# A recurrent attention loop with streamed weights: new fixed order, V and O in parts, mask on TensorE, half of the KT and QT copies on ScalarE

## The chip, the cores and the metric

The kernel runs on one core of one Trainium2 chip. The time is the device time of a whole execution in microseconds (us). All runs told here are fast; each is compared by its ratio to runs of the kernel before of the same rounds on the same chip. The profile is one execution taken by the hardware profiler.

In this kernel TensorE does the matmuls and transposes and writes them to PSUM; VectorE (DVE in the profile), ScalarE (ACT) and GpSimd (POOL) copy and compute on tiles; SyncE (SP) issues the loads of the weights into SBUF, the on-chip memory. PE in the profile is a matmul, PEld the load of its stationary operand.

## The reference, cut to what matters

Two independent parts are concatenated. Part A (a short convolution and a long one by FFT) is not touched by the change. Part B is recurrent over 64 segments:

```python
for s in range(n_seg):                       # 64 segments of 32 tokens
    h = concat([mem, xs])                    # 8 + 32 = 40 rows, 1024 wide
    q, k, v = h @ Wq, h @ Wk, h @ Wv         # 32 heads of 128
    p = softmax(where(mask, q @ k.T * scale, -1e9))
    o = (p @ v) @ Wo
    mem = o[:, :8]                           # goes into the next segment
    outs.append(o[:, 8:])
```

A segment needs all four weight matrices, 32 MB in bf16, and the next segment needs its result. The mask lets memory rows see everything and is causal otherwise.

## The kernel before

The weights are 64 chunks of 128 x 2048 bf16 (512 KB). 44 stay in SBUF, 20 are streamed again in every segment through a ring of four slots. A slot is loaded again when TensorE is done with it:

```python
NSTREAM = 20        # chunks streamed per segment
RING = 4
...
    def fetch():
        n = len(loaded)
        if n < len(uses):
            t = ring.tile([128, 2048], BF, tag="wring", name="wring")
            nc.sync.dma_start(dst_view(t[:], uses[n]), dram_chunk(uses[n]))
            loaded.append(t)
    ...
    def done(ch):                 # after the matmuls of a chunk
        if ch in streamed:
            loaded[used[0]] = None
            used[0] += 1
            fetch()
```

The heads are done in two halves (g = 0, 1). KT and QT are the transposed keys and queries, S the scores, PT the transposed probabilities, OT the attention output, `acc` and `yacc` the sums of the projections. The order of a segment is fixed by the program text; each engine works its own instructions in that order (the timeline below shows it on VectorE: a copy stands behind a softmax that it does not need, and TensorE waits 1.45 us):

```python
            k0 = evac_qk(proj(0, 0))            # K, half 0: 8 chunks, then a ScalarE copy
            q0 = evac_qk(proj(1, 0))
            KT0 = keys(0)
            transposes(k0, KT0[:, :, :, 0:32])  # TensorE transposes, VectorE copy to SBUF
            k1 = evac_qk(proj(0, 1))
            ...
            transposes(q0, QT0[:])
            q1 = evac_qk(proj(1, 1))
            S0 = scores(0, QT0, KT0)
            PT0 = softmax(S0)                   # VectorE chain with Exp on ScalarE
            KT1 = keys(1)
            transposes(k1, KT1[:, :, :, 0:32])  # its VectorE copy stands behind softmax(S0)
            a_v0 = proj(2, 0)
            ...
            transposes(q1, QT1[:])
            S1 = scores(1, QT1, KT1)
            a_v1 = proj(2, 1)
            ...
            attend(0, PT0, V0, OTp)
            evac_o(0, OTp, OT0)
            ...
            PT1 = softmax(S1)
            ...
            out_proj(0, ...)                    # 8 chunks of Wo, needs OT0 at once
            attend(1, PT1, V1, OTp)
            evac_o(1, OTp, OT1)
            out_proj(1, ...)                    # needs OT1 at once
            Y = ...                             # copy, two transposes, copy into `rec`: the next h
```

There is one PSUM buffer for transposes (`tp`), so the transposes of q1 wait until KT1 was copied out. The softmax works on 4 x 2 blocks of 40 columns: per block of heads one block for the recurrent 32 rows and one, a quarter filled, for the last 8 tokens of a segment:

```python
            def softmax(S):
                nc.vector.scalar_tensor_tensor(out=S4, in0=S4, scalar=scale, in1=mask[...],
                                               op0=ALU.mult, op1=ALU.add)       # mask pass
                nc.vector.tensor_reduce(out=mx[:], in_=S3, op=ALU.max, axis=AX.X)
                nc.vector.tensor_tensor(out=S3, in0=S3, in1=mx[...], op=ALU.subtract)
                nc.scalar.activation(S3, S3, ACT.Exp)
                ... # sum, reciprocal, multiply into P_pad, two 32x32-block transposes into PT
```

## Time and profile before

The median before the change was 2918.79 us (three runs, 2917.12 to 2920.53). The loop over the segments takes 80% of it. The copies of Y on ScalarE mark the segments: the first ends at 603.0 us, the last at 2904.3 us, so a segment takes (2904.3 - 603.0) / 63 = 36.5 us.

| per segment, kernel before | us |
|---|---|
| TensorE busy | 24.6 |
| TensorE idle until a weight load has landed | 6.2 |
| TensorE idle for another engine or its own queue | 5.7 |
| sum | 36.5 |

These are sums over all segments but the first and last five. The waits themselves, in the view of waits for TensorE between 1500 and 2500 us (27.4 segments; the columns are us in total, times, and the longest in us):

```profile
PE acc L616 <- DMA wring<-in_B_Wq_dram: 132.4, 112, 2.8
PE yacc L695 <- ACT OT L683: 43.0, 56, 1.1
PE qk_tp L630 <- DVE KT L631: 36.1, 28, 2.1
PE OTp L673 <- DVE PT L663: 34.4, 21, 2.1
PE acc L616 <- DMA wring<-in_B_Wv_dram: 21.6, 31, 1.6
PE S L637 <- DVE QT L631: 14.5, 28, 0.5
PE y_tp L581 <- ACT Y L741: 12.1, 27, 0.5
PE acc L616 <- DMA wring<-in_B_Wk_dram: 9.3, 11, 1.8
PE acc L616 <- DVE rec L582: 9.2, 27, 0.3
PE yacc L695 <- DMA wring<-in_B_Wo_dram: 6.8, 10, 1.7
```

The rows with `wring` are the weight ring, 170 us in all. OT, KT, PT and QT are dependencies that another order could cover, 128 us or 4.7 us a segment. Y and `rec` are the hand-over to the next segment, which nothing can cover. How the KT wait comes about is seen in the timeline (start, duration, engine; in brackets the idle time before and what ended it):

```profile
1535.92 0.77 DVE L663 STREAM_TRANSPOSE PT<-P_pad 128x256 bf16<-128x256 bf16 x2
1536.62 0.38 DVE L631 COPY KT<-qk_tp 128x512 bf16<-128x512 bf16 x1
1537.06 0.38 PE L630 MATMUL qk_tp<-ident,qk_sb 128*128 128x128 bf16 x4 [1.45 <-DVE KT L631]
```

The copy of KT could have been made long before. It stood behind the end of the softmax (the last transposes into PT are seen) on VectorE, and TensorE waited 1.45 us for the transpose buffer. The same wait one segment earlier took 2.04 us:

```profile
1499.97 0.45 PE L630 MATMUL qk_tp<-ident,qk_sb 128*128 128x128 bf16 x4 [2.04 <-DVE KT L631]
```

The windows view gives, for a stretch, its length, the busy time of PE, PEld, DVE, ACT and POOL, then the granted TensorE clock, the busy share of the DMA engines and the GB/s. First the whole loop, then two single microseconds just after that wait:

```profile
700.00:2500.00 1800.00, 1210.35 (x24686) 639.10 (x24682) 458.14 (x1150) 286.32 (x543) 230.84 (x495) 0.85 0.88 298
...
1501.00:1502.00 1.00, 1.00 (x40) 0.50 (x44) 0.00 (x0) 0.00 (x0) 0.00 (x0) 0.50 1.01 395
1502.00:1503.00 1.00, 1.00 (x16) 0.42 (x12) 0.00 (x0) 0.00 (x0) 0.00 (x0) 0.50 0.41 152
```

While TensorE was held up it freed no slot, so SyncE issued no load of the ring between 1497.8 and 1502.3 us. The loads under way land, and the DMA falls from 395 to 152 GB/s in a microsecond in which TensorE is busy again, here at half clock. Later TensorE catches up and starves. The time from issue to landing of the ring's loads, from the view of the tile `wring` over 1500 to 2500 us:

```profile
DMA to landing us min/median/max: 3.8/5.6/8.2
```

(The trace has the landing of three ring loads in eight.) With 20 loads a segment and 5.6 us each, 20 x 5.6 / 36.5 = 3.1 of the four slots are under way on average.

### The profile page before, as it was taken

To read this page: it belongs to the slowest core of one execution; us is meant where nothing else is said; L and a number is where in the kernel's file an instruction comes from. 1 tells how busy PE (TensorE), PEld (TensorE's weight loads), DVE (VectorE), ACT (ScalarE), POOL (GpSimd) and SP (SyncE) were. 2 spreads that over 40 slices of the span, in tenths; PEclk is the share of its full clock that TensorE was granted. 3 is DMA by queue.
4 is the path that set the end of the run, shared out by engine and by line. 5 is a ranking of instruction groups with operands and counts; after the bars stand their busy time and mean duration, and the time that the engine had idled before them with its cause. 6 is when DMAs were issued, how large, how long until landed. Compare 5 with 4: busy or idle time off the path is not lost. (4 is left out here: it accounts for less than half of the span.)

```text
span 2915.3 us, 75121 instructions
## 1 busy us (share of the span) xinstructions
PE 1911.7 (66%) x33470; PEld 975.6 (33%) x33492; DVE 847.1 (29%) x1940; ACT 577.1 (20%) x1015; POOL 382.4 (13%) x742
## 2 busy tenths in 40 slices
PE   3664698366666666676666666666667666766765
PEld 1221343133333333333333333333333333333333
DVE  6894211022222222222222222222222222222222
ACT  6771111011111111111111111111111111111111
POOL 4141000011111111111111111111111111111111
PEclk9797698688888988888888888888887888788888
DMA  7887655888888888888888889888888888888896
GB/s 244 297 268 277 235 137 164 293 297 293 300 294 302 306 303 295 298 296 299 298 300 288 299 298 315 289 298 297 304 302 301 296 294 292 308 297 292 304 304 227
DMA packets 340398, 830.98 MB, mean 285 GB/s; under 512 B 72076, under 2 KB 84396, under 8 KB 340071
## 3 DMA queue, kind: packets, MB, share of 16 engines
q1 hardware_dynamic: 306520, 767.19, 77.2%
q0 software_dynamic: 23168, 34.77, 3.7%
q10 hardware_dynamic: 10384, 24.20, 2.5%
q8 instruction: 262, 4.29, 0.6%
q14 instruction: 64, 0.52, 0.1%
HBM read 774.52 MB, written 51.38 MB: 283 GB/s over the span
## 5 line engine op out<-in xcount | busy, mean ns | idle before, releaser
L616 PE MATMUL acc<-wring,rec 128*32 128x512 bf16 x3840 | 453.2, 457 | 410.1 <-DMA wring<-in_B_Wq_dram 301.4
L616 PEld LDWEIGHTS <-rec 128*32 128x32 bf16 x12288 | 365.4, 108 | 945.6 <-issue 738.8
L616 PE MATMUL acc<-Wearly,rec 128*32 128x512 bf16 x4608 | 440.8, 465 | 32.8 <-DVE rec L582 21.7
L695 PE MATMUL yacc<-Wlate,OT 128*32 128x256 bf16 x5632 | 307.7, 320 | 97.8 <-ACT OT L683 97.7
L616 PE MATMUL acc<-Wlate,rec 128*32 128x512 bf16 x3840 | 352.7, 438 | 0.0
L624 ACT CAST qk_sb<-acc 128x512 bf16<-128x512 f32 x256 | 149.8, 585 | 1016.9 <-PE acc L616 960.9
L695 PEld LDWEIGHTS <-OT 128*32 128x32 bf16 x8192 | 250.1, 113 | 163.5 <-ACT OT L683 111.4
L631 DVE COPY KT<-qk_tp 128x512 bf16<-128x512 bf16 x128 | 51.8, 404 | 583.5 <-PE qk_tp L630 583.5
L683 ACT CAST OT<-OTp 128x512 bf16<-128x512 f32 x128 | 74.9, 585 | 525.9 <-PE OTp L677 525.9
L630 PE MATMUL qk_tp<-ident,qk_sb 128*128 128x128 bf16 x1024 | 115.7, 244 | 91.1 <-DVE KT L631 91.1
L695 PE MATMUL yacc<-wring,OT 128*32 128x256 bf16 x2560 | 164.8, 325 | 13.6 <-DMA wring<-in_B_Wo_dram 12.4
L684 DVE CAST OTB<-OTp 128x128 bf16<-128x128 f32 x128 | 37.4, 292 | 365.9 <-ACT OT L683 365.9
L574 POOL DMA_DIRECT2D rec<-REC x64 | 37.2, 581 | 810.3 <-PE OTp L677 562.3
L606 POOL COPY KT<-rec 128x128 bf16<-128x128 bf16 x128 | 38.1, 298 | 796.0 <-PE S L641 708.6
L648 DVE SCALAR_TENSOR_TENSOR S<-S,mask 128x320 f32<-128x320 f32 x128 | 63.3, 495 | 239.5 <-PE S L641 239.5
L630 PEld LDWEIGHTS <-qk_sb 128*128 128x128 bf16 x1024 | 71.0, 106 | 183.9 <-issue 175.9
L744 POOL DMA_DIRECT2D out_dram<-Y x64 | 48.2, 752 | 636.3 <-ACT Y L741 588.2
L602 POOL DMA_DIRECT2D VBs<-VBD x256 | 129.2, 511 | 0.3
L631 DVE COPY QT<-qk_tp 128x512 bf16<-128x512 bf16 x128 | 54.3, 424 | 237.6 <-PE qk_tp L630 237.6
L673 PE MATMUL OTp<-PT,V 32*128 32x40 bf16 x2048 | 55.3, 180 | 80.1 <-DVE PT L663 78.7
L663 DVE STREAM_TRANSPOSE PT<-P_pad 128x256 bf16<-128x256 bf16 x256 | 98.7, 424 | 4.4
L695 PE MATMUL ybacc<-Wlate,OTB 128*32 128x256 bf16 x1408 | 92.4, 289 | 5.3 <-ACT V L728 2.7
(258 smaller groups left out, 2090.4 us busy)
## 6 DMA issues: line engine op xcount, KB each, us to landing
wring<-in_B_Wq_dram SPq DMA_DIRECT2D x384, 512.0 KB, 5.4
wring<-in_B_Wv_dram SPq DMA_DIRECT2D x320, 512.0 KB, 5.8
wring<-in_B_Wo_dram SPq DMA_DIRECT2D x320, 512.0 KB, 5.4
wring<-in_B_Wk_dram SPq DMA_DIRECT2D x256, 512.0 KB, 6.1
rec<-REC POOLq DMA_DIRECT2D x64, 192.0 KB, 5.7
SK_61<-s_sb SPq DMA_DIRECT2D x16, 512.0 KB, 4.4
SU_60<-s_sb SPq DMA_DIRECT2D x16, 512.0 KB, 3.7
Kg<-SK_61 ACTq DMA_DIRECT2D x32, 256.0 KB, 4.7
```

The source lines that it names most:

```text
L602: nc.gpsimd.dma_start(VBs[32 * c:32 * c + 8, :], VBD[s, c])
L606: nc.gpsimd.tensor_copy(KT[:, :, :, 32:40], KBs[:, 128 * g:128 * g + 128].rearrange("p (c i t) -> p i c t", c=4, i=4))
L616: nc.tensor.matmul(acc[32 * c:32 * c + 32, :], lhsT=hT[:, kc, :], rhs=w[:, c * 512:(c + 1) * 512], start=(kc == 0), stop=(kc == 7), tile_p ...
L624: nc.scalar.copy(sb[:], acc[:])
L630: nc.tensor.transpose(tp[:, i * 128:(i + 1) * 128], sb[:, i * 128:(i + 1) * 128], ident[:])
L631: nc.vector.tensor_copy(dst, tp[:].rearrange("p (i c r) -> p i c r", i=4, c=4))
L648: nc.vector.scalar_tensor_tensor(out=S4, in0=S4, scalar=scale, in1=mask[:].unsqueeze(1).to_broadcast([128, 4, 2, 40]), op0=ALU.mult, op1=A ...
L663: nc.vector.transpose(out=PT[:, kb].rearrange("p i (a q) -> p (i a) q", a=2), in_=P_pad[:].rearrange("p i a k -> p (i a) k")[:, :, 32 * kb ...
L673: nc.tensor.matmul(OTp[:, c, idx * 40:idx * 40 + 40], lhsT=V[32 * c:32 * c + 32, cv], rhs=PT[32 * c:32 * c + 32, 0, i, 0:40], start=True, ...
L683: nc.scalar.copy(OT[:], v[:, :, :, 0:32])
L695: nc.tensor.matmul(acc[32 * dq:32 * dq + 32, 0:256], lhsT=src[:, c, idx, :], rhs=w[:, hh * 1024 + dq * 256:hh * 1024 + (dq + 1) * 256], st ...
L744: nc.gpsimd.dma_start(bass.AP(outb.tensor, outb.offset + SEG * s * 2048, [[256, 4], [2048, 32], [1, 256]]), Y[:])
```

## The change

The intent: make the loop's order such that TensorE always has matmuls to do while another engine works on what it needs next, and shorten the softmax. It does five things:

1. V is projected in parts (2 + 3 + 3 chunks, 4 + 4 chunks) and Wo too (5, then 3 + 8), with transposes, scores and attends between the parts.
2. The mask is added by TensorE: a matmul of the identity with the mask opens the accumulation of the scores. The scale moves into Exp.
3. The last 8 queries of four heads are packed in one score block: 5 blocks of 40 columns in place of 8. Both halves then share one PSUM tile.
4. Half 1's KT and QT are copied out of PSUM by ScalarE.
5. The streamed Wo chunks are first copied to contiguous rows (WOS), so that their loads have runs of 4 KB, not 2 KB. The title does not name this.

The diff holds smaller things too: the copies of q, k and V and the OT tiles share three rotating buffers, the output of the last tokens accumulates in the other half of `yacc`, and a memset of `rec` on GpSimd is gone.

```diff
+    WOS = dram.tile([max(1, len(ostream)), 128, 2048], BF, name="WOS")
+    for i, ch in enumerate(ostream):
+        nc.gpsimd.dma_start(WOS[i].rearrange("p (hh d) -> p hh d", hh=2), dram_chunk(ch))
@@ fetch
-            nc.sync.dma_start(dst_view(t[:], uses[n]), dram_chunk(uses[n]))
+            nc.sync.dma_start(t[:], stream_src(uses[n]))
@@ scores (cut)
+                nc.tensor.matmul(S.rearrange("p b k -> p (b k)"), lhsT=ident[:],
+                                 rhs=mask[:].rearrange("p b k -> p (b k)"), start=True, stop=False)
...
-                        nc.tensor.matmul(S[32 * c:32 * c + 32, i, 1, :], lhsT=QBs[:, o:o + 32], rhs=KT[:, i, c, :],
-                                         start=True, stop=True, tile_position=(0, 32 * c))
+                        nc.tensor.matmul(S[32 * c:32 * c + 32, 4, :], lhsT=QBm[:, c, i, :], rhs=KT[:, i, c, :],
+                                         start=False, stop=(i == 3), tile_position=(0, 32 * c))
@@ order of a segment (cut)
-            S0 = scores(0, QT0, KT0)
-            PT0 = softmax(S0)
-            KT1 = keys(1)
-            transposes(k1, KT1[:, :, :, 0:32])
-            a_v0 = proj(2, 0)
-            nc.scalar.copy(V0[:], a_v0[:])
-            transposes(q1, QT1[:])
-            S1 = scores(1, QT1, KT1)
-            a_v1 = proj(2, 1)
+            scores(0, QT0, KT0, Sp[:, 0])
+            pv0 = Proj(2, 0).run(2)
+            KT1 = keys(1)
+            last_queries(1)                     # GpSimd: 4 small copies into QBm
+            nc.scalar.copy(KT1[:, :, :, 0:32], transposes(k1))
+            softmax_a(Sp[:, 0])                 # max, subtract, Exp
+            PT0 = softmax_b(Sp[:, 0])           # sum, reciprocal, multiply, transposes
+            pv0.run(3)
+            nc.scalar.copy(QT1[:], transposes(q1))
+            pv0.run(3)
+            V0 = pv0.evac()
+            scores(1, QT1, KT1, Sp[:, 1])
+            softmax_a(Sp[:, 1])
+            pv1 = Proj(2, 1).run(4)
             attend(0, PT0, V0, OTp)
-            evac_o(0, OTp, OT0)
+            OT0 = evac_o(0)
+            PT1 = softmax_b(Sp[:, 1])
+            evac_ob(0)
+            pv1.run(4)
...
-            out_proj(0, list(zip((OT0, OTB), accs)))
+            out_proj(range(0, 5), OT0)
             attend(1, PT1, V1, OTp)
-            evac_o(1, OTp, OT1)
-            out_proj(1, list(zip((OT1, OTB), accs)))
+            OT1 = evac_o(1)
+            evac_ob(1)
+            out_proj(range(5, 8), OT0)
+            out_proj(range(8, 16), OT1)
```

More of the change, by code (lines that the diff above doesn't have):

```diff
@@ L418, in b_kernel @@
     late = resident[NEARLY:]
+    ostream = [ch for ch in order if ch[0] == 3 and ch in streamed]
     def dram_chunk(ch):
@@ L425, in dst_view, with stream_src @@
         return ap.rearrange("p (hh d) -> p hh d", hh=2) if ch[0] == 3 else ap
+    def stream_src(ch):
+        return WOS[ostream.index(ch)] if ch[0] == 3 else dram_chunk(ch)
     dram = ctx.enter_context(tc.tile_pool(name="b_dram", bufs=1, space=DRAM))
@@ L434, in b_kernel @@
     make_identity(nc, ident[:])
-    mask = const.tile([128, 2, 40], BF, name="mask")
+    mask = const.tile([128, 5, 40], BF, name="mask")
     wres = ctx.enter_context(tc.tile_pool(name="b_wres", bufs=1))
@@ L450, in b_kernel @@
         nc.vector.tensor_copy(rowi[:], rowi_i[:])
+        rowb_i = tmpc.tile([128, 1], I32, name="rowb_i")
+        nc.vector.tensor_scalar(out=rowb_i[:], in0=rowi_i[:], scalar1=7, scalar2=None, op0=ALU.bitwise_and)
+        rowb = tmpc.tile([128, 1], F32, name="rowb")
+        nc.vector.tensor_copy(rowb[:], rowb_i[:])
         ismem = tmpc.tile([128, 1], F32, name="ismem")
@@ L459, in b_kernel @@
         nc.vector.memset(ok[:, 1, 0:32], 1.0)
-        nc.vector.tensor_scalar(out=ok[:, 1, 32:40], in0=coli[:, 0:8], scalar1=rowi[:, 0:1], scalar2=None, op0=ALU.is_le)
-        nc.vector.tensor_scalar(out=mask[:], in0=ok[:], scalar1=-1.0, scalar2=-NEG, op0=ALU.add, op1=ALU.mult)
+        nc.vector.tensor_scalar(out=ok[:, 1, 32:40], in0=coli[:, 0:8], scalar1=rowb[:, 0:1], scalar2=None, op0=ALU.is_le)
+        nc.vector.tensor_scalar(out=mask[:, 0:4, :], in0=ok[:, 0:1, :].to_broadcast([128, 4, 40]),
+                                scalar1=-1.0, scalar2=-NEG / scale, op0=ALU.add, op1=ALU.mult)
+        nc.vector.tensor_scalar(out=mask[:, 4, :], in0=ok[:, 1, :], scalar1=-1.0, scalar2=-NEG / scale,
+                                op0=ALU.add, op1=ALU.mult)
     with ExitStack() as c0:
@@ L539, in b_kernel @@
     two = ctx.enter_context(tc.tile_pool(name="b_two", bufs=2))
+    rot = ctx.enter_context(tc.tile_pool(name="b_rot", bufs=3))
     ps_acc = ctx.enter_context(tc.tile_pool(name="b_ps_acc", bufs=2, space=PSUM))
@@ L566, in done @@
             fetch()
-    P_pad = one.tile([128, 4, 2, 64], BF, name="P_pad")
+    P_pad = one.tile([128, 5, 64], BF, name="P_pad")
     nc.vector.memset(P_pad[:], 0.0)
+    QBm = one.tile([128, 4, 4, 32], BF, name="QBm")
+    nc.vector.memset(QBm[:], 0.0)
     pend = {}
     def load_x(s):
-        rec = one.tile([128, 800], BF, tag="rec", name="rec")
-        nc.gpsimd.dma_start(rec[:, 0:768], REC[:, s, :])
-        nc.gpsimd.memset(rec[:, 768:800], 0.0)
-        pend[s] = (rec[:, 0:256].rearrange("p (k t) -> p k t", k=8), rec[:, 256:512], rec[:, 512:800])
+        rec = one.tile([128, 768], BF, tag="rec", name="rec")
+        nc.gpsimd.dma_start(rec[:], REC[:, s, :])
+        pend[s] = (rec[:, 0:256].rearrange("p (k t) -> p k t", k=8), rec[:, 256:512], rec[:, 512:768])
     def fill_mem(hT, Y):
@@ L608, in keys, with last_queries, __init__, run @@
                 return KT
-            def proj(m, g):
-                acc = ps_acc.tile([128, 512], F32, tag="acc", name="acc")
-                for kc in range(8):
-                    ch = (m, kc, g)
-                    w = weight(ch)
-                    for c in range(4):
-                        nc.tensor.matmul(acc[32 * c:32 * c + 32, :], lhsT=hT[:, kc, :],
-                                         rhs=w[:, c * 512:(c + 1) * 512],
-                                         start=(kc == 0), stop=(kc == 7), tile_position=(0, 32 * c))
-                    done(ch)
-                return acc
-            def evac_qk(acc):
-                sb = two.tile([128, 512], BF, tag="qk", name="qk_sb")
-                nc.scalar.copy(sb[:], acc[:])
-                return sb
-            def transposes(sb, dst):
+            def last_queries(g):
+                q = QBm[:].rearrange("p c i w -> p c (i w)")
+                for i in range(4):
+                    nc.gpsimd.tensor_copy(
+                        q[:, :, 40 * i:40 * i + 8],
+                        QBs[:, 128 * g:128 * g + 128].rearrange("p (c i t) -> p c i t", c=4, i=4)[:, :, i, :])
+            class Proj:
+                def __init__(self, m, g):
+                    self.m, self.g, self.kc = m, g, 0
+                    self.acc = ps_acc.tile([128, 512], F32, tag="acc", name="acc")
+                def run(self, n=8):
+                    for kc in range(self.kc, self.kc + n):
+                        ch = (self.m, kc, self.g)
+                        w = weight(ch)
+                        for c in range(4):
+                            nc.tensor.matmul(self.acc[32 * c:32 * c + 32, :], lhsT=hT[:, kc, :],
+                                             rhs=w[:, c * 512:(c + 1) * 512],
+                                             start=(kc == 0), stop=(kc == 7), tile_position=(0, 32 * c))
+                        done(ch)
+                    self.kc += n
+                    return self
+                def evac(self):
+                    sb = rot.tile([128, 512], BF, tag="rot", name="qkv_sb")
+                    nc.scalar.copy(sb[:], self.acc[:])
+                    return sb
+            def transposes(sb):
                 tp = ps_t.tile([128, 512], BF, tag="tp", name="qk_tp")
@@ L630, in transposes, with scores @@
                     nc.tensor.transpose(tp[:, i * 128:(i + 1) * 128], sb[:, i * 128:(i + 1) * 128], ident[:])
-                nc.vector.tensor_copy(dst, tp[:].rearrange("p (i c r) -> p i c r", i=4, c=4))
-            def scores(g, QT, KT):
-                S = ps_s.tile([128, 4, 2, 40], F32, tag="S", name="S")
+                return tp[:].rearrange("p (i c r) -> p i c r", i=4, c=4)
+            def scores(g, QT, KT, S):
+                nc.tensor.matmul(S.rearrange("p b k -> p (b k)"), lhsT=ident[:],
+                                 rhs=mask[:].rearrange("p b k -> p (b k)"), start=True, stop=False)
@@ L635, in scores @@
                 for i in range(4):
                     for c in range(4):
-                        nc.tensor.matmul(S[32 * c:32 * c + 32, i, 0, :], lhsT=QT[:, i, c, :], rhs=KT[:, i, c, :],
-                                         start=True, stop=True, tile_position=(0, 32 * c))
+                        nc.tensor.matmul(S[32 * c:32 * c + 32, i, :], lhsT=QT[:, i, c, :], rhs=KT[:, i, c, :],
+                                         start=False, stop=False, tile_position=(0, 32 * c))
                     for c in range(4):
-                        o = (16 * g + 4 * c + i) * 8
@@ L641, in scores @@
-                        nc.tensor.matmul(S[32 * c:32 * c + 32, i, 1, :], lhsT=QBs[:, o:o + 32], rhs=KT[:, i, c, :],
-                                         start=True, stop=True, tile_position=(0, 32 * c))
-                return S
-            def softmax(S):
-                S4 = S[:]
-                S3 = S[:].rearrange("p i a k -> p (i a) k")
-                nc.vector.scalar_tensor_tensor(out=S4, in0=S4, scalar=scale,
-                                               in1=mask[:].unsqueeze(1).to_broadcast([128, 4, 2, 40]),
-                                               op0=ALU.mult, op1=ALU.add)
-                mx = two.tile([128, 8], F32, tag="mx", name="mx")
-                nc.vector.tensor_reduce(out=mx[:], in_=S3, op=ALU.max, axis=AX.X)
-                nc.vector.tensor_tensor(out=S3, in0=S3, in1=mx[:].unsqueeze(2).to_broadcast([128, 8, 40]),
+                        nc.tensor.matmul(S[32 * c:32 * c + 32, 4, :], lhsT=QBm[:, c, i, :], rhs=KT[:, i, c, :],
+                                         start=False, stop=(i == 3), tile_position=(0, 32 * c))
@@ L654, in softmax, with softmax_a @@
+            def softmax_a(S):
+                mx = two.tile([128, 5], F32, tag="mx", name="mx")
+                nc.vector.tensor_reduce(out=mx[:], in_=S, op=ALU.max, axis=AX.X)
+                nc.vector.tensor_tensor(out=S, in0=S, in1=mx[:].unsqueeze(2).to_broadcast([128, 5, 40]),
                                         op=ALU.subtract)
-                nc.scalar.activation(S3, S3, ACT.Exp)
-                ssum = two.tile([128, 8], F32, tag="ssum", name="ssum")
-                nc.vector.tensor_reduce(out=ssum[:], in_=S3, op=ALU.add, axis=AX.X)
+                nc.scalar.activation(S, S, ACT.Exp, scale=scale)
@@ L658, in softmax, with softmax_b @@
+            def softmax_b(S):
+                ssum = two.tile([128, 5], F32, tag="ssum", name="ssum")
+                nc.vector.tensor_reduce(out=ssum[:], in_=S, op=ALU.add, axis=AX.X)
                 nc.vector.reciprocal(ssum[:], ssum[:])
-                nc.vector.tensor_tensor(out=P_pad[:].rearrange("p i a k -> p (i a) k")[:, :, 0:40], in0=S3,
-                                        in1=ssum[:].unsqueeze(2).to_broadcast([128, 8, 40]), op=ALU.mult)
-                PT = one.tile([128, 2, 4, 64], BF, tag="PT", name="PT")
+                nc.vector.tensor_tensor(out=P_pad[:, :, 0:40], in0=S,
+                                        in1=ssum[:].unsqueeze(2).to_broadcast([128, 5, 40]), op=ALU.mult)
+                PT = one.tile([128, 2, 4, 40], BF, tag="PT", name="PT")
@@ L662, in softmax @@
                 for kb in range(2):
-                    nc.vector.transpose(out=PT[:, kb].rearrange("p i (a q) -> p (i a) q", a=2),
-                                        in_=P_pad[:].rearrange("p i a k -> p (i a) k")[:, :, 32 * kb:32 * kb + 32])
+                    ks = slice(32 * kb, 32 * kb + 32)
+                    nc.vector.transpose(out=PT[:, kb, :, 0:32], in_=P_pad[:, 0:4, ks])
+                    nc.vector.transpose(out=PT[:, kb, :, 32:40], in_=P_pad[:, 4, ks])
                 return PT
@@ L673, in attend @@
                         nc.tensor.matmul(OTp[:, c, idx * 40:idx * 40 + 40], lhsT=V[32 * c:32 * c + 32, cv],
-                                         rhs=PT[32 * c:32 * c + 32, 0, i, 0:40], start=True, stop=False,
+                                         rhs=PT[32 * c:32 * c + 32, 0, i, :], start=True, stop=False,
                                          tile_position=(32 * c, 0))
@@ L677, in attend, with o_view, evac_o, evac_ob @@
                         nc.tensor.matmul(OTp[:, c, idx * 40:idx * 40 + 40], lhsT=VBs[32 * c:32 * c + 8, cs],
-                                         rhs=PT[32 * c:32 * c + 8, 1, i, 0:40], start=False, stop=True,
+                                         rhs=PT[32 * c:32 * c + 8, 1, i, :], start=False, stop=True,
                                          tile_position=(32 * c, 0))
-            def evac_o(g, OTp, OT):
-                v = OTp[:, :, 160 * g:160 * g + 160].rearrange("p c (i q) -> p c i q", i=4)
-                nc.scalar.copy(OT[:], v[:, :, :, 0:32])
-                nc.vector.tensor_copy(OTB[:, :, 4 * g:4 * g + 4, 8 * j:8 * j + 8], v[:, :, :, 32:40])
-            def out_proj(g, pairs):
-                for hp in range(8 * g, 8 * g + 8):
+            def o_view(g):
+                return OTp[:, :, 160 * g:160 * g + 160].rearrange("p c (i q) -> p c i q", i=4)
+            def evac_o(g):
+                OT = rot.tile([128, 4, 4, 32], BF, tag="rot", name="OT")
+                nc.scalar.copy(OT[:], o_view(g)[:, :, :, 0:32])
+                return OT
+            def evac_ob(g):
+                nc.vector.tensor_copy(OTB[:, :, 4 * g:4 * g + 4, 8 * j:8 * j + 8], o_view(g)[:, :, :, 32:40])
+            def out_proj(hps, OT):
+                for hp in hps:
                     ch = (3, hp, 0)
@@ L691, in out_proj @@
                         h = 2 * hp + hh
-                        c, i = (h % 16) // 4, h % 4
-                        for src, acc, idx in ((pairs[0] + (i,)), *(p + (4 * g + i,) for p in pairs[1:])):
+                        g, c, i = h // 16, (h % 16) // 4, h % 4
+                        lhs = [(OT[:, c, i, :], 0)]
+                        if j == NB - 1:
+                            lhs.append((OTB[:, c, 4 * g + i, :], 256))
+                        for src, o in lhs:
                             for dq in range(4):
-                                nc.tensor.matmul(acc[32 * dq:32 * dq + 32, 0:256], lhsT=src[:, c, idx, :],
+                                nc.tensor.matmul(yacc[32 * dq:32 * dq + 32, o:o + 256], lhsT=src,
                                                  rhs=w[:, hh * 1024 + dq * 256:hh * 1024 + (dq + 1) * 256],
-                                                 start=(h == 0), stop=(h == 31), tile_position=(0, 32 * dq))
+                                                 start=(h == 0 and o == 0), stop=(h == 31 and o == 0),
+                                                 skip_group_check=(o > 0), tile_position=(0, 32 * dq))
                     done(ch)
@@ L701, in b_kernel @@
                 OTB = one.tile([128, 4, 8, 32], BF, tag="OTB", name="OTB")
-            k0 = evac_qk(proj(0, 0))
-            q0 = evac_qk(proj(1, 0))
+            Sp = ps_s.tile([128, 2, 5, 40], F32, tag="S", name="S")
+            OTp = ps_o.tile([128, 4, 512], F32, tag="OTp", name="OTp")
+            k0 = Proj(0, 0).run().evac()
+            q0 = Proj(1, 0).run().evac()
             KT0 = keys(0)
-            transposes(k0, KT0[:, :, :, 0:32])
-            k1 = evac_qk(proj(0, 1))
+            last_queries(0)
@@ L707, in b_kernel @@
+            nc.vector.tensor_copy(KT0[:, :, :, 0:32], transposes(k0))
+            k1 = Proj(0, 1).run().evac()
             QT0 = one.tile([128, 4, 4, 32], BF, tag="QT", name="QT")
-            transposes(q0, QT0[:])
-            q1 = evac_qk(proj(1, 1))
-            S0 = scores(0, QT0, KT0)
-            PT0 = softmax(S0)
+            nc.vector.tensor_copy(QT0[:], transposes(q0))
+            q1 = Proj(1, 1).run().evac()
+            scores(0, QT0, KT0, Sp[:, 0])
+            pv0 = Proj(2, 0).run(2)
@@ L712, in b_kernel @@
             KT1 = keys(1)
-            transposes(k1, KT1[:, :, :, 0:32])
-            a_v0 = proj(2, 0)
-            V0 = one.tile([128, 512], BF, tag="V", name="V")
-            nc.scalar.copy(V0[:], a_v0[:])
-            QT1 = one.tile([128, 4, 4, 32], BF, tag="QT", name="QT")
-            transposes(q1, QT1[:])
-            S1 = scores(1, QT1, KT1)
-            a_v1 = proj(2, 1)
+            last_queries(1)
+            nc.scalar.copy(KT1[:, :, :, 0:32], transposes(k1))
+            softmax_a(Sp[:, 0])
@@ new lines, in b_kernel @@
+            PT0 = softmax_b(Sp[:, 0])
+            pv0.run(3)
+            QT1 = one.tile([128, 4, 4, 32], BF, tag="QT", name="QT")
+            nc.scalar.copy(QT1[:], transposes(q1))
[4 more added lines that the diff above has]
+            pv1 = Proj(2, 1).run(4)
+            attend(0, PT0, V0, OTp)
+            OT0 = evac_o(0)
+            PT1 = softmax_b(Sp[:, 1])
+            evac_ob(0)
+            pv1.run(4)
@@ L721, in b_kernel @@
             if s + 1 < n_seg:
                 load_x(s + 1)
-            OTp = ps_o.tile([128, 4, 512], F32, tag="OTp", name="OTp")
-            attend(0, PT0, V0, OTp)
-            OT0 = one.tile([128, 4, 4, 32], BF, tag="OT", name="OT")
-            evac_o(0, OTp, OT0)
-            V1 = one.tile([128, 512], BF, tag="V", name="V")
-            nc.scalar.copy(V1[:], a_v1[:])
-            PT1 = softmax(S1)
-            yacc = ps_acc.tile([128, 512], F32, tag="acc", name="yacc")
-            accs = [yacc]
@@ L732, in b_kernel @@
-            if j == NB - 1:
-                ybacc = ps_acc.tile([128, 512], F32, tag="acc", name="ybacc")
-                accs.append(ybacc)
-            out_proj(0, list(zip((OT0, OTB), accs)))
+            V1 = pv1.evac()
+            yacc = ps_acc.tile([128, 512], F32, tag="acc", name="yacc")
+            out_proj(range(0, 5), OT0)
             attend(1, PT1, V1, OTp)
-            OT1 = one.tile([128, 4, 4, 32], BF, tag="OT", name="OT")
-            evac_o(1, OTp, OT1)
-            out_proj(1, list(zip((OT1, OTB), accs)))
+            OT1 = evac_o(1)
@@ L746, in b_kernel @@
                 YB = two.tile([128, 256], BF, tag="Y", name="YB")
-                nc.vector.tensor_copy(YB[:], ybacc[:, 0:256])
+                nc.vector.tensor_copy(YB[:], yacc[:, 256:512])
                 for dq in range(4):
```

## The prediction

> **What bounds it now.** The 64 segments fill about 566 to 2905 us; the copies of Y (timeline of ScalarE) come every 36.5 us. The rest is untouched but for five DMAs. Per segment, from the view of waits over 1500 to 2500 us (27.4 segments), TensorE is busy about 24.6 us and idle for two kinds of reason:
> - the weight ring: `acc` and `yacc` behind `wring` loads, 132.4 + 21.6 + 9.3 + 6.8 = 170 us, 6.2 us a segment;
> - small dependencies: transposes behind the KT copy (queued behind softmax on VectorE) 36.1, attend behind PT 34.4, out-projection behind OT 43.0, scores behind QT 14.5: 128 us, 4.7 us a segment; also Y and `rec`, about 0.8 us.
>
> They take turns: while TensorE waits for VectorE, the four ring slots fill and the DMA idles; later TensorE starves. The windows view shows it: DMA share 0.88 and 298 GB/s on average, falling to 0.4 in single microseconds. A segment streams 20 x 512 KB. With loads queued, landings follow each other 1.27 us apart at best and about 1.6 us on average (small DMAs of VBs, rec and Y in between): 32 to 33 us a segment. That floor stays.
>
> TensorE's clock is 0.5 in whole 3.41 us steps after stretches with under about 45% busy, mean 0.85.[...]
>
> **What the change does.**
> - Removes the mask pass (VectorE, 0.49 us, twice) and shrinks 320 columns to 200: passes and Exp from 0.42-0.50 to an estimated 0.3-0.36; softmax from about 4.2 to about 2.9 us.
> - Adds a 128x200 mask matmul per half (estimated 0.1 us[...]), and eight small GpSimd copies a segment (estimated 0.2 us each, off the path).
> - Moves half 1's KT and QT copies to ScalarE (0.58 us each), past softmax; splits V and O so that matmuls cover PT, OT and the transposes. By the new order, PT of half 0 has about 4 us of TensorE work over it, PT of half 1 about 3, OT 0.65 to 0.9.
> - Copies five Wo chunks once into contiguous rows (estimated 0 to 5 us: the engines wait for ScalarE's tables until 40 us then), and streams them as 4 KB packets, not 2 KB. Packets took 84 ns (2 KB) and 159 ns (4 KB) at the median: at most 5% on a quarter of the stream.
>
> **On the critical path.** About 4.2 of the 4.7 us of dependencies go. The DMA becomes the sole limit: ring waits should grow from 6 to 9-10 us a segment, and the gain stops at the streaming floor. I put the segment at 32.8 us: 3.7 x 64 = 237 us less, plus about 10 us for what I missed: 2695 us. Range 2610 to 2795. Chances: faster by over 2% 0.94, same 0.05, slower 0.01.
>
> **Right if:** Y copies every 32-33.5 us; DMA share 0.94 or more, 325-335 GB/s; waits on KT, PT, OT each under 0.4 us a segment; `wring` waits 9 us or more; mean clock 0.85 to 0.93; VectorE busy down by about 100 us or more.
>
> **Wrong if:** a ring of four cannot keep the DMA full even with a steady TensorE (then about 34.5 us, 2790); load spacing is near its best 1.27 us when never interrupted (about 30 us, under 2600); starving keeps TensorE at half clock and makes it the limit; ScalarE, now with both copies and Exp, delays QT or OT; or the Wo copies hold up part A's loads.

The sum: 36.5 - 32.8 = 3.7 us a segment, 3.7 x 64 = 237 us off 2918.79 us and 10 us added make about 2692 us, put as 2695 us. What the trace of the kernel before shows: four transposes by the identity took 0.38 us, 0.10 us each (the mask matmul), and a GpSimd copy of 128x128, four times a new one's size, 298 ns. TensorE stood idle for 24.7 us behind ScalarE until 40.56 us (the Wo copies). Between 700 and 2500 us, 105 of 116 falls to half clock came after 3.41 us with under 45% of matmul busy time.

## The result, and the profile after

The changed kernel took 2760.45 us at the median (2754.92 to 2771.43, four runs), against 2917.95 us before in four runs. A ratio here and below is the mean time of a kernel's fast runs over that of the other's fast runs of the same rounds, so not quite the ratio of these medians: 0.947, with a 95% interval of 0.9434 to 0.9506. This is 65 us above the predicted 2695 us and inside the range.

The profiled execution took 2752.4 us. Its Y copies end at 599.4 us and 2740.9 us: (2740.9 - 599.4) / 63 = 34.0 us a segment, 2.5 us less than before. Of the 163 us between the two profiled spans, 160 lie between the first and the last Y copy. The same view of waits for TensorE, 1500 to 2500 us (29.4 segments):

```profile
PE acc L649 <- DMA wring<-in_B_Wq_dram: 121.7, 116, 3.1
PE yacc L735 <- DMA wring<-WOS: 63.8, 83, 2.5
PE acc L649 <- DMA wring<-in_B_Wv_dram: 46.5, 71, 2.5
PE acc L649 <- DMA wring<-in_B_Wk_dram: 30.3, 31, 3.2
PE yacc L735 <- issue: 14.6, 13, 1.8
PE y_tp L601 <- ACT Y L785: 13.7, 29, 0.5
PE acc L649 <- DVE rec L602: 9.8, 29, 0.3
```

OT, KT, PT and QT are gone from the list. What remains is the weight ring, 262 us or 8.9 us a segment where it was 6.2, the hand-over, and 0.5 us a segment before the first Wo matmuls for which the view shows no releaser (`issue`). The timeline shows the cover at work: KT goes out on ScalarE beside the softmax, and TensorE has a chunk of V at every place.

```profile
1530.24 0.40 PE L664 MATMUL qk_tp<-ident,qkv_sb 128*128 128x128 bf16 x4
...
1530.36 0.38 DVE L681 TENSOR_TENSOR S<-S,mx 128x200 f32<-128x200 f32 x1
...
1530.57 0.40 PE L649 MATMUL acc<-Wlate,rec 128*32 128x512 bf16 x4
1530.72 0.59 ACT L758 COPY KT<-qk_tp 128x512 bf16<-128x512 bf16 x1 [0.69 <-DVE S L681]
...
1531.36 0.38 PE L664 MATMUL qk_tp<-ident,qkv_sb 128*128 128x128 bf16 x4
```

No idle time stands before either transpose. The windows view of the loop, and the landing of the ring's loads:

```profile
700.00:2500.00 1800.00, 1255.06 (x26489) 632.47 (x26480) 336.30 (x1233) 359.58 (x689) 305.26 (x904) 0.91 0.92 321
```

```profile
DMA to landing us min/median/max: 4.3/6.0/8.2
```

So 20 x 6.0 / 34.0 = 3.5 slots are now under way. The DMA does more, 321 GB/s at a share of 0.92, but a share of 0.92 is not the full DMA that was expected once TensorE no longer waits for anything else. That gap is what the experiments are about.

### The profile page after: what moved, and what is told of

It reads as the page before. It is cut to its first block, busy times and chain, and to the rows that moved or that the text cites. A ratio compares the mean times of both kernels' runs of the same rounds, so it can differ in the third digit from the quotient of the medians.

```text
span 2752.4 us, 76238 instructions
## 1 busy us (share of the span) xinstructions
PE 1851.6 (67%) x33620; PEld 910.9 (33%) x33620; DVE 662.9 (24%) x1944; ACT 639.9 (23%) x1143; POOL 454.2 (17%) x1195
## 5 line engine op out<-in xcount | busy, mean ns | idle before, releaser
L649 PE MATMUL acc<-wring,rec 128*32 128x512 bf16 x3840 | 419.9, 425 | 455.5 <-DMA wring<-in_B_Wq_dram 261.0
L649 PEld LDWEIGHTS <-rec 128*32 128x32 bf16 x12288 | 341.0, 102 | 932.9 <-issue 727.9
L658 ACT CAST qkv_sb<-acc 128x512 bf16<-128x512 f32 x384 | 225.1, 586 | 1143.8 <-PE acc L649 1095.7
L649 PE MATMUL acc<-Wearly,rec 128*32 128x512 bf16 x4608 | 425.8, 451 | 34.7 <-DVE rec L602 23.6
L735 PE MATMUL yacc<-Wlate,OT 128*32 128x256 bf16 x5632 | 280.6, 292 | 11.4 <-issue 11.4
L749 DVE COPY KT<-qk_tp 128x512 bf16<-128x512 bf16 x64 | 27.2, 425 | 549.8 <-PE qk_tp L664 549.8
L680 DVE TENSOR_REDUCE mx<-S 128x5 f32<-128x200 f32 x128 | 47.1, 368 | 281.9 <-PE S L675 281.1
L664 PE MATMUL qk_tp<-ident,qkv_sb 128*128 128x128 bf16 x1024 | 110.2, 235 | 0.0
L785 ACT CAST Y<-yacc 128x256 bf16<-128x256 f32 x64 | 23.8, 373 | 356.8 <-PE yacc L735 356.8
L664 PEld LDWEIGHTS <-qkv_sb 128*128 128x128 bf16 x1024 | 63.5, 103 | 113.8 <-issue 83.8
L735 PE MATMUL yacc<-Wlate,OTB 128*32 128x256 bf16 x1408 | 91.2, 276 | 11.7 <-issue 11.3
L721 DVE CAST OTB<-OTp 128x128 bf16<-128x128 f32 x128 | 34.8, 272 | 246.3 <-ACT OT L717 246.3
L529 PE MATMUL kb_ps<-XBT,Wearly 128*128 128x512 bf16 x288 | 84.3, 384 | 1.2 <-ACT XBT L498 1.2
```

The lines of the kernel that those rows point to most:

```text
L529: nc.tensor.matmul(ps[:], lhsT=ws[kc][:, hl * 128:(hl + 1) * 128], rhs=XBT[:, kc].rearrange("p s t -> p (s t)"), start=(kc == 0), stop=(kc ...
L649: nc.tensor.matmul(self.acc[32 * c:32 * c + 32, :], lhsT=hT[:, kc, :], rhs=w[:, c * 512:(c + 1) * 512], start=(kc == 0), stop=(kc == 7), t ...
L658: nc.scalar.copy(sb[:], self.acc[:])
L664: nc.tensor.transpose(tp[:, i * 128:(i + 1) * 128], sb[:, i * 128:(i + 1) * 128], ident[:])
L680: nc.vector.tensor_reduce(out=mx[:], in_=S, op=ALU.max, axis=AX.X)
L721: nc.vector.tensor_copy(OTB[:, :, 4 * g:4 * g + 4, 8 * j:8 * j + 8], o_view(g)[:, :, :, 32:40])
```

## The experiments

My theory at this point: the new order made the gain, by taking the dependencies away; the remaining limit is the stream of weights. Its rivals: the shorter softmax, the ScalarE copies or the 4 KB runs made it; and, for the limit, that TensorE itself or the DMA engines' capacity holds the kernel, or that a ring of four slots does.

### One part undone at a time

**e1_no_wos.** Wo is streamed from its own place again:

```diff
-        return WOS[ostream.index(ch)] if ch[0] == 3 else dram_chunk(ch)
+        return dram_chunk(ch)
-            nc.sync.dma_start(t[:], stream_src(uses[n]))
+            nc.sync.dma_start(dst_view(t[:], uses[n]), stream_src(uses[n]))
```

> The changed kernel, but the five streamed Wo chunks are read from Wo itself again (2 KB runs), without the copy. Theory (hiding the dependencies made the gain, packet size is a side matter): 2765 to 2800 us, at most 0.6 us more a segment, all of it in the landings of Wo chunks. Rival (the larger packets made most of the gain): 2850 us or more.

Measured: 2765.66 us, ratio to before 0.949 (0.945 to 0.953), against 0.947 for the changed kernel. As the theory had it: the copy to contiguous rows is worth nothing that these runs show. In this run's loop a 2 KB packet of SyncE's queue took 92.9 ns on average and a 4 KB one 186.7 ns, the same per byte (84 and 159 ns at the median).

**e2_old_order.** The loop in the order of before, everything else of the change kept:

```diff
-            pv0 = Proj(2, 0).run(2)
+            softmax_a(Sp[:, 0])
+            PT0 = softmax_b(Sp[:, 0])
             ... (KT1 by ScalarE)
+            V0 = Proj(2, 0).run().evac()
             ... (QT1 by ScalarE, scores of half 1)
-            pv1 = Proj(2, 1).run(4)
+            pv1 = Proj(2, 1).run()
             attend(0, PT0, V0, OTp)
             ...
+            softmax_a(Sp[:, 1])
+            PT1 = softmax_b(Sp[:, 1])
-            out_proj(range(0, 5), OT0)
+            out_proj(range(0, 8), OT0)
             attend(1, PT1, V1, OTp)
-            out_proj(range(5, 8), OT0)
```

> The changed kernel with the loop's old order: whole V projections and whole output projections, attend 0 after V of half 1; the mask on TensorE, the packing, the ScalarE copies and the contiguous Wo stay. Theory (order is the main part): waits on PT and OT come back, about 2.5 us of dependencies a segment, partly paid by fewer weight waits: 2825 to 2880 us. Rival (shorter softmax and ScalarE copies do it by themselves): 2760 to 2790 us.

Measured: 2803.47 us, ratio 0.9593 (0.9557 to 0.963). This lies between the two expectations, so neither held: the order by itself is worth only 1.3% on top of the rest (0.9593 / 0.947). The waits that came back are those on OT and QT, not those on KT and PT:

```profile
PE yacc L735 <- ACT OT L717: 44.5, 56, 0.8
PE acc L649 <- DMA wring<-in_B_Wk_dram: 41.0, 40, 2.7
PE acc L649 <- DMA wring<-in_B_Wv_dram: 38.5, 53, 1.9
PE S L672 <- ACT QT L762: 24.5, 29, 1.1
...
PE OTp L704 <- DVE PT L695: 3.9, 5, 0.9
```

**e3_old_softmax.** Mask pass on VectorE, 320 columns, one score buffer; order, copies and WOS as changed. The scores, the softmax and the mask are those of the kernel before, split in softmax_a (up to Exp) and softmax_b:

```diff
-                nc.tensor.matmul(S..., lhsT=ident[:], rhs=mask[...], start=True, stop=False)
+                S = ps_s.tile([128, 4, 2, 40], F32, tag="S", name="S")
 ...
+                nc.vector.scalar_tensor_tensor(out=S[:], in0=S[:], scalar=scale, in1=mask[...],
+                                               op0=ALU.mult, op1=ALU.add)
```

> The changed kernel with the old scores and softmax: mask by a VectorE pass, 320 columns, one score buffer for both halves; new order, ScalarE copies and contiguous Wo stay. Theory (new order hides even the longer chain, the stream is the limit): 2760 to 2795 us. Rival (the shorter chain is what the new order needs): PT waits of over 1 us a segment and 2830 us or more.

Measured: 2745.64 us, ratio 0.9412 (0.9375 to 0.945), a shade better than the changed kernel, with intervals that just overlap. The theory's direction held and its range was too high: under the new order the packed, TensorE-masked softmax gains nothing. It costs TensorE a little (23.8 us busy a segment against 23.3 here) and saves 0.3 us of waits on the score buffer. Under the old order it may be worth something; see e12.

**e4_dve_copies.** Half 1's KT and QT copies on VectorE:

```diff
-            nc.scalar.copy(KT1[:, :, :, 0:32], transposes(k1))
+            nc.vector.tensor_copy(KT1[:, :, :, 0:32], transposes(k1))
-            nc.scalar.copy(QT1[:], transposes(q1))
+            nc.vector.tensor_copy(QT1[:], transposes(q1))
```

> The changed kernel with half 1's KT and QT copies on VectorE, where the QT copy queues behind the whole softmax of half 0. Theory: scores of half 1 wait about 1 us a segment more, of which the stream swallows half: 2770 to 2805 us. Rival (the move to ScalarE is worth nothing): 2750 to 2768 us.

Measured: 2791.18 us, ratio 0.9555 (0.9526 to 0.9585). As the theory had it. The score matmuls of half 1 wait again, and ring waits fall by nearly as much (8.8 to 7.8 us, other waits 1.5 to 2.7):

```profile
PE S L672 <- DVE QT L763: 20.9, 29, 0.8
...
PE S L668 <- DVE P_pad L689: 12.9, 19, 0.8
```

**e12_before_actcopies.** The other way round: the kernel before with these two copies moved, and nothing else.

```diff
-            def transposes(sb, dst):
+            def transposes(sb, dst, copy=nc.vector.tensor_copy):
-            transposes(k1, KT1[:, :, :, 0:32])
+            transposes(k1, KT1[:, :, :, 0:32], nc.scalar.copy)
-            transposes(q1, QT1[:])
+            transposes(q1, QT1[:], nc.scalar.copy)
```

> The kernel before with half 1's KT and QT copies on ScalarE, nothing else. Theory (this is a large part of what the old order with everything else gained): the KT wait of 1.36 us a segment goes, the period falls by 0.4 to 0.9 us: 2860 to 2895 us. Rival (it is the shorter softmax that gained it): 2905 us or more.

Measured: 2850.44 us, ratio 0.9777 (0.973 to 0.9824), even below the theory's range. Moving two copies to an engine that is mostly idle (ScalarE was busy 20% of the span) gives 2.2% of the change's 5.3%. The KT wait is gone and 14 of the 34 us of PT wait with it:

```profile
PE yacc L695 <- ACT OT L683: 42.7, 56, 0.8
PE acc L616 <- DMA wring<-in_B_Wk_dram: 25.7, 30, 3.0
PE S L637 <- ACT QT L631: 22.6, 28, 0.9
PE OTp L673 <- DVE PT L663: 20.0, 20, 2.1
...
PE qk_tp L630 <- ACT KT L631: 1.0, 5, 0.2
```

From here to e2, which has the old order too, is another 1.9% (0.9777 to 0.9593), and the PT wait falls from 20.0 to 3.9 us. The new softmax, WOS or the smaller things of the diff made that; no run separates them under the old order.

The parts do not add up: undone one at a time they cost 0.2% (e1), 1.3% (e2), -0.6% (e3) and 0.9% (e4), 1.8% of the 5.3%. Where a dependency is left in, ring waits are shorter (7.4 us in e2, 7.8 in e4, 8.8 without). That led to the ring.

### What the rest waits for

**e5_ns21_r4** and **e6_ns21_r5.** One chunk more is streamed and one less is resident; in e6 the freed 4 KB per partition become a fifth slot. (20 chunks with five slots did not build: the pool `b_rot` wanted 3 KB per partition and 0.06 KB were left.)

```diff
-NSTREAM = 20
+NSTREAM = 21
-RING = 4
+RING = 5          # e6 only
```

> The changed kernel with 21 instead of 20 weight chunks streamed a segment, ring of four. Theory (the stream is the limit, about 1.65 us a chunk): 105 us more than the changed kernel, 2850 to 2880 us, ratio to before about 0.982. Rival (TensorE and its dependencies are the limit): under 30 us more.

> 21 chunks streamed, ring of five (the same memory as 20 and four). Theory (a ring of four leaves the queue short part of the time; that is why a segment took 34.0 us and not 32.8): 35 to 80 us less than with 21 and four. Rival (the DMA engines themselves, with the small DMAs, are at their capacity): within 12 us of 21 and four.

Measured: e5 took 2853.82 us, ratio 0.979 (0.9748 to 0.9833), 35.5 us a segment: a streamed chunk costs about 1.6 us a segment, as expected of a stream-limited loop. Windows view and landings of e5:

```profile
700.00:2500.00 1800.00, 1245.75 (x25374) 615.26 (x25373) 320.67 (x1175) 343.14 (x657) 291.66 (x863) 0.89 0.92 323
```

```profile
DMA to landing us min/median/max: 3.7/5.8/8.5
```

e6 took 2586.18 us, ratio 0.888 (0.8843 to 0.8917): 268 us less than e5, by nothing but the fifth slot, and three times what I had expected at most. The segment fell to 31.3 us while it loads 5% more than the changed kernel. Windows view and landings of e6:

```profile
700.00:2500.00 1800.00, 1323.97 (x28818) 664.77 (x28821) 367.47 (x1346) 391.98 (x751) 331.66 (x986) 0.96 0.98 366
```

```profile
DMA to landing us min/median/max: 3.6/6.5/9.1
```

21 x 6.5 / 31.3 = 4.4 loads are under way where it was 3.5; each takes a little longer to land (6.5 us, was 6.0), but the sum of them is faster. The same engines move 366 GB/s. So the DMA's capacity was not what held the changed kernel; the number of loads that may be under way was. Nearly every slot is in loading: 3.5 of four, 4.4 of five, so only about half a slot on average holds weights that wait for TensorE or are in use.

**e10_ns22_r6.** One step further, 22 chunks and six slots.

> The changed kernel with 22 chunks streamed and a ring of six. Theory (five slots already fill the DMA, share 0.98, about 1.49 us a chunk): a chunk more costs about 1.4 us a segment, 2650 to 2690 us. Rival (latency still limits at five): 2590 us or less.

Measured: 2580.23 us, ratio 0.8841 (0.8803 to 0.8878). The theory failed and the rival held: five slots did not fill the DMA, a share of 0.98 or not. A chunk more costs no time, so a chunk went from 31.29 / 21 = 1.49 us (e6) to 31.35 / 22 = 1.43 us:

```profile
700.00:2500.00 1800.00, 1334.22 (x28798) 668.38 (x28798) 366.25 (x1345) 390.82 (x750) 325.66 (x974) 0.94 1.00 382
```

```profile
DMA to landing us min/median/max: 3.7/7.6/10.4
```

From four slots to six the GB/s rose by 19%, the busy share only by 9% (0.92 to 1.00). The rest is that packets became quicker: between 700 and 2500 us a 4 KB packet of SyncE's queue took 185 ns on average in the changed kernel, 173 in e6 and 170 in e10. Why was not tested; a busy share near 1 is thus no proof of a full DMA: after e6's 0.98 still 4% were to be had (382 over 366 GB/s).

**e9_before_r5.** 21 chunks and five slots in the kernel before, nothing else.

> The kernel before with 21 chunks streamed and a ring of five, nothing else. Theory (at four slots both kernels were held by how many loads can be under way; a fifth helps each of them, but the old order keeps its 4.7 us of dependencies a segment): 2640 to 2740 us, between the changed kernel and the changed kernel with five slots. Rival (the kernel before was held by its dependencies, the ring only matters once they are gone): 2860 us or more, as there is one chunk more to load.

Measured: 2783.06 us, ratio 0.9534 (0.949 to 0.9578). Between the two expectations: the ring helps the old order too, by nearly as much as the whole change does, but its dependencies stay and then bind:

```profile
...
PE yacc L695 <- ACT OT L683: 44.4, 58, 0.8
PE OTp L673 <- DVE PT L663: 37.7, 21, 2.1
...
PE qk_tp L630 <- DVE KT L631: 26.0, 24, 2.0
```

With five slots the change is worth 0.888 / 0.9534 = 0.931, so 6.9%, more than the 5.3% with four. The two together (0.888) save more than their product (0.947 x 0.9534 = 0.903): each makes the other worth more, and neither replaces the other.

**e7_pe_pad.** 24 more mask matmuls a segment, each overwritten by the next, so that the result stays right:

```diff
-                nc.tensor.matmul(S..., lhsT=ident[:], rhs=mask[...], start=True, stop=False)
+                for n in range(13):
+                    nc.tensor.matmul(S..., lhsT=ident[:], rhs=mask[...], start=True, stop=(n < 12))
```

> The changed kernel with 12 more mask matmuls per half (24 a segment, about 2 to 2.6 us of TensorE work; the result is the same). Theory (TensorE has slack behind the stream): under 0.8 us a segment, so less than 50 us more. Rival (TensorE is as much a limit): 1.5 us a segment or more, at least 100 us more.

Measured: 2794.45 us, ratio 0.9588 (0.9542 to 0.9635). The theory held. TensorE was busy 25.6 us a segment, 1.8 more (2 to 2.6 us was an estimate; in the changed kernel's timeline four transposes by the same identity take 0.40 us, and 24 x 0.10 = 2.4 us), and the segment took 0.75 us more; ring waits fell from 8.8 to 7.6 us. TensorE has slack, but not all of what is added is hidden. A late TensorE also frees slots late (3.3 loads under way, not 3.5); that this is the reason was not tested.

**e8_small_sp.** The small DMAs (VBs and `rec`, the inputs of a segment; Y and YB, its outputs) issued by SyncE, which also issues the ring's loads (`nc.gpsimd.dma_start` becomes `nc.sync.dma_start` in four places).

> The changed kernel with the small DMAs of the loop (VBs, rec, Y and YB) issued from SyncE's queue, not from GpSimd. Theory (in the first half of a segment the slow landings, 1.8 to 2.6 us for streamed chunks 4 and 5 against 1.3 to 1.5 us, come from these DMAs): they shrink and 0.5 to 1 us a segment goes: 2700 to 2730 us. Rival (what they cost is the bytes and not the path, or SyncE stalls the ring behind them): 2755 us or more.

Measured: 2848.39 us, ratio 0.9779 (0.9744 to 0.9813). The rival held. In the queue's own waits SyncE stands behind the stores of YB, up to 4.9 us, and issues no weights meanwhile:

```profile
SPq L793 <- DMA out_dram<-Y: 27.1, 7, 4.9
```

Every fourth segment, the one after those stores, took 38.6 us, where the changed kernel's took 33.8 us: 4.8 / 4 = 1.2 of the 1.4 us by which a segment became longer. Whether the small DMAs slow the stream by themselves is left open.

**e11_best.** e6 with the softmax of e3.

> The changed kernel with 21 chunks and a ring of five, and with the old scores and softmax of the third experiment (mask by VectorE, 320 columns). Theory (the stream is the limit, the softmax's form plays no part): within 1% of 2586 us. Rival (with the stream faster, the longer softmax chain is no longer covered): 2620 us or more, with PT waits of over 0.7 us a segment.

Measured: 2588.22 us, ratio 0.8853 (0.8807 to 0.8899). As the theory had it: the form of the softmax plays no part here either. The versions that clearly beat both kernels are thus e6, e10 and e11, all within 0.4% of each other.

All runs side by side. The last six columns are worked out from each run's trace over all segments but the first and last five: us per segment, and the mean number of ring loads between issue and landing, worked out for all loads from the three in eight whose landing the trace has. Of e8 it has none.

| run | median us | ratio to before | period | PE busy | ring waits | other waits | loads under way | GB/s |
|---|---|---|---|---|---|---|---|---|
| before | 2917.95 | 1 | 36.5 | 24.6 | 6.2 | 5.7 | 3.2 | 299 |
| changed | 2760.45 | 0.947 | 34.0 | 23.8 | 8.8 | 1.5 | 3.5 | 321 |
| e1 no WOS | 2765.66 | 0.949 | 34.0 | 23.6 | 9.0 | 1.4 | 3.5 | 321 |
| e2 old order | 2803.47 | 0.959 | 34.8 | 23.8 | 7.4 | 3.5 | 3.3 | 313 |
| e3 old softmax | 2745.64 | 0.941 | 33.9 | 23.3 | 8.7 | 1.8 | 3.5 | 322 |
| e4 VectorE copies | 2791.18 | 0.956 | 34.5 | 24.0 | 7.8 | 2.7 | 3.4 | 316 |
| e12 before, ScalarE copies | 2850.44 | 0.978 | 35.5 | 24.0 | 7.4 | 4.1 | 3.3 | 307 |
| e7 padded TensorE | 2794.45 | 0.959 | 34.7 | 25.6 | 7.6 | 1.7 | 3.3 | 313 |
| e8 small DMAs on SyncE | 2848.39 | 0.978 | 35.4 | 24.1 | 9.8 | 1.5 | - | 308 |
| e5 21 chunks, ring 4 | 2853.82 | 0.979 | 35.5 | 24.6 | 9.4 | 1.4 | 3.5 | 322 |
| e9 before, 21, ring 5 | 2783.06 | 0.953 | 34.6 | 23.7 | 5.4 | 5.5 | 3.9 | 330 |
| e6 21, ring 5 | 2586.18 | 0.888 | 31.3 | 23.0 | 6.5 | 1.7 | 4.4 | 365 |
| e11 21, ring 5, old softmax | 2588.22 | 0.885 | 31.6 | 22.9 | 6.7 | 2.0 | 4.4 | 362 |
| e10 22, ring 6 | 2580.23 | 0.884 | 31.4 | 23.3 | 5.9 | 2.2 | 5.3 | 382 |

Read it by the column of loads under way: the GB/s follow it in every row, through changes of order, of slots and of work on TensorE. By itself this shows no cause, as loads under way are the rate times the time to landing; e5 against e6 shows it, where only the slots differ.

## Why the prediction was right or wrong, point by point

The time was inside the range and the direction clear, but the gain was sized 223 us and came out at 158 us. The range also held the case that the prediction listed as making it wrong (2790 us), so being inside it does not tell the two apart.

- *Dependencies go.* Right. "About 4.2 of the 4.7 us" were to go; KT, PT, OT and QT are gone from the waits, and other waits fell from 5.7 to 1.5 us a segment.
- *The ring takes part of it back.* Right in kind and nearly in size: 9 to 10 us expected, 8.8 us found. Before, it was 6.2 us.
- *The segment takes 32.8 us.* Wrong; 34.0 us. This is the term that was mis-sized: 3.7 x 64 = 237 us was predicted, (36.5 - 34.0) x 64 = 160 us came. The prediction had also not added up its own parts: 24.6 us busy, 9 to 10 us of ring and about 1.3 us of other waits make 35 to 36 us, not 32.8. That TensorE would be busy a little less, 23.8 us at a clock of 0.91, it had not costed.
- *"That floor stays": 32 to 33 us a segment.* This is the step that failed. The average of 1.6 us between queued landings was read as what the DMA can do. It was what the DMA did with three to four loads under way, so it was no floor. Nor did four slots reach it with the dependencies gone: 34.0 / 20 = 1.70 us a chunk. With five slots a chunk takes 1.49 us and with six 1.43 us, small DMAs included, and the clean 1.27 us stood in the same trace. The prediction named the true limit among what would make it wrong: "a ring of four cannot keep the DMA full even with a steady TensorE (then about 34.5 us, 2790)". e6 shows that this is what happened.
- *DMA share 0.94 or more, 325 to 335 GB/s.* Wrong: 0.92 and 321 GB/s, for the same reason.
- *The 10 us for what was missed.* Not needed: the loop starts no later than before (first Y copy at 599.4 us, was 603.0), so the Wo copies at the start cost nothing that is seen.
- *4 KB packets gain at most 5% of a quarter of the stream.* Right as a bound; e1 shows no gain.
- *The softmax shortens to 2.9 us.* In the segment shown it took from 1529.95 to 1533.29 us on VectorE, 3.3 us; the passes take 0.37 us where 0.3 to 0.36 was estimated, and the four smaller transposes take longer (0.92 us) than the two they replace (0.85 us, twice the 424 ns mean). It hardly matters, as e3 shows: under the new order even the old chain is covered.
- *A mask matmul of 0.1 us.* Too low. The matmul took 0.26 us at the median, twice a segment, and stood behind 0.34 us without a load of its stationary operand (19.9 us before 58 of them). What these 0.34 us are was not shown.
- *GpSimd's copies, 0.2 us each off the path.* Right: 210 ns on average, and no engine waits for them. VectorE's busy time fell by 847.1 - 662.9 = 184 us; over 100 us were expected.
- *Clock 0.85 to 0.93.* Right: 0.897 over the span. In the traces the clock is whole or half: between 700 and 2500 us of the changed kernel it changes 154 times, always at whole multiples of 3.413 us from one another. Of its 77 falls half came after 3.41 us with 40% or more of matmul busy time, up to 57%; and it rose again after 81% or more. Others with as little as 44% kept the full clock, so the profile's matmul busy time alone gives no exact threshold, and the prediction's "under about 45%" describes most falls (61 of the 77), not all.

What I first held to be the main part, the order, is 1.3% of the 5.3% when all else is in place, and the copies on ScalarE are 0.9% in place and 2.2% alone. What one part is worth depends on which others are in, so a share of the gain cannot be given to each. Shown is that, with the new order, the softmax's new form and WOS are each not needed for it.

Why is one slot worth 9%? The quickest ring loads of these traces took 3.6 us (e6) to 4.3 us (changed kernel) from issue to landing. The landings themselves most often follow each other 1.27 us apart: in the kernel before, between 700 and 2500 us, a quarter of the distances lie between 1.25 and 1.30 us. Even the quickest load thus holds its slot for about three times the 1.27 us, and then the slot waits for TensorE to use it. With four slots and TensorE using them unevenly, 3.5 were under way. The number of loads under way over the landing time is the rate: 3.5 / 6.0 us is one chunk in 1.7 us, and 4.4 / 6.5 us one in 1.5 us. What makes up the time of the quickest load, or the time above it when more are under way, was not shown.

## What to carry to other kernels

Take away first the waits that are only a place in a queue: a copy behind an unrelated chain on another engine's queue costs a few lines to move and was the cheapest 2% here. Before calling a stream of loads the floor, divide: loads under way over the time from issue to landing gives its rate, and if the slots are few, another slot is worth trying even at the price of more bytes to load. And add up busy time and all waits to the predicted period: if they don't make it, one of them is wrong.
